# A recurrent attention layer feeding a soft mixture of experts: a reordered unit loop, spread-out tables, and another order at the end

## The chip, the cores and the metric

The kernel runs on one core of a Trainium2 chip. A core has a matrix engine (PE), a vector engine (DVE), a scalar engine (ACT), a general engine (POOL) and a queue engine (SP) that only issues transfers. Each engine works through its own list of instructions in order and waits at semaphores for the others. Sixteen DMA engines move data between the chip's memory (HBM) and the core's on-chip memory (SBUF); transfers are issued by SP or by POOL here. Results of PE land in banks of a small memory (PSUM), which the kernel names T0, T1, Ab, Mb, Yb, Xb and Vb, and are carried off by DVE or ACT.

The metric is the device time of one execution in microseconds (us), the median of several runs. For the kernel before it is 124.12 us over 6 runs (123.98 to 125.6).

## The reference, cut to what matters

The first half is a recurrent attention with a decaying state. `w` is the decay per head and channel, `u` a bonus for the current position. The second half takes the result as tokens, mixes them softly into 32 slots, sends four slots through each of eight experts, and mixes the slots' results back to the tokens.

```
# B, H, S, D = 4, 8, 768, 48;  N, Dm, E, F = 3072, 384, 8, 1024;  32 slots
for t in range(S):
    cur = einsum('bhd,bhe->bhde', u * k[t], v[t])
    y[t] = einsum('bhd,bhde->bhe', r[t], state + cur)
    state = w * state + einsum('bhd,bhe->bhde', k[t], v[t])
x = y as (3072, 384)
logits = x @ phi                           # (3072, 32)
d = softmax of logits over the 3072 tokens # dispatch
slot_input = d.T @ x                       # 32 slots, 4 of each expert
slot_out[e] = relu(slot_input[e] @ w1[e]) @ w2[e]
c = softmax of logits over the 32 slots    # combine
out = c @ slot_out                         # (3072, 384), float32
```

## The kernel before

**Units and iterations.** A unit is one batch and one pair of heads: 4 x 4 = 16 units. The sequence of 768 positions is cut into six chunks of 128, three in each half, so that there are 32 half-units. The main loop `for i in range(-5, nH)` works on half-units; `mu` is i // 2, and odd and even iterations do different things. It is software pipelined: in iteration i one finds the output of half-unit i (`y_pe`, `y_evac`), the diagonal products and the state of half-unit i+1 (`a_pe`, `mask_f`, `m_pe`, `z_evac`), the reordering of v for half-unit i+2 (`v_pe`, `v_evac`), and the preparation of unit mu+2 and of unit mu+3.

**What a unit needs.** POOL multiplies k and r (float32, as loaded) by tables W of powers of the decay (`scale`, L228; unit 0 on DVE). PE transposes the six blocks of k into bank T0 in the even iteration and those of r into bank T1 in the odd one (`t_pe`, L235). ACT carries them off as kT and rT (`t_evac`, L241). PE transposes kT back into T0 (`b_pe`, L247), and DVE carries that off as kn (`b_evac`, L252). DVE multiplies r from T1 by kT as `prod` (`prod_f`, L257), which is needed for the term with u. PE multiplies kT by rT into bank Ab (`a_pe`, L299), and DVE masks that to the causal triangle as AT (`mask_f`, L304). PE forms the state of three chunks and, behind it, the sums with u into bank Mb (`m_pe`, L314 to L329). DVE carries the state off as Z, masked to the two heads' blocks with `bmask` (`z_evac`, L343); for the first half of a unit also as Z0, multiplied by the decay over 384 positions (L339); and multiplies v by the sums as dv (L345). PE adds AT by v, rT by Z, and dv in bank Yb (`y_pe`, L355 to L368), and ACT writes that to x (`y_evac`, L375).

**Routing.** Once a batch is done, `route` takes it through the mixture in the following iterations: transposes of x, logits, their exponential Le, the dispatch sums (`disp`, L425 and L429) in a corner of bank T1, which DVE adds to `acc` in the same iteration (`disp_ev`, L434 and L436), and the transposed exponentials LexpT.

**Order.** All instructions go through `O(...)`, which keeps the order of the program on each engine. Nothing is planned: what the source says first is what an engine does first. Memory hazards become semaphore waits by themselves.

**Transfers.** SP issues k, r and v of batches 0 and 1 in pieces of two heads, then phi, then batch 2, and in iteration 3 batch 3, which goes into the buffer of batch 0. POOL issues the expert weights (`load_w`) from iteration 13 on, as `W_AT` says, between its `scale` steps: w1 of the eight experts, then w2. A weight of 1.5 MB in float32 is converted to bfloat16 on its way. w2 goes to the buffers of batches 1 and 2; that of the last expert comes in three pieces.

**Tables.** `tt` (DVE, L182) and `ex` (ACT, L186) make the eight tables W, one for k or r and a pair of heads; four of them before the loop, the rest in its first iterations by `T_AT`. POOL clears `bmask`, `ones`, `ucol`, `Le`, `uns` ahead of the loop and forms `ucol` from w and u.

**The end.** After the loop come the logits of the last half batches, the first layer of the experts (L594), its transposes (L617), the row sums of the combining softmax in three parts (`row_sums`, L608 and L610), the second layer with all four experts of a group in one pass (L627), the scaling to `so` (L631, L632), and 24 products with LexpT, each carried off by DVE or ACT in turn (L646 to L650) and written out in groups of 1, 1, 2, 4, 4, 4, 4, 4 blocks of 128 tokens (L652).

Of the kernel before, what the change touches and what calls it, by code (L numbers as in the profile page):

```python
# [9 lines left out]
def kernel(  # L10
# [87 lines left out]
    warm = LexpT[:, 2048:2560]  # L98
    wu = cst.tile([8, 128], f32, name="wu")
    wu3 = wu[:].rearrange("q (e s) -> q e s", s=64)  # L100
    phi_f = cst.tile([128, nM, ES], f32, name="phi_f")
    O(act.preload_act_table_set("natural_log_exp_and_others"))
    O(sp.dma_start(out=w_row, in_=w.rearrange("(o h) d -> o (h d)", o=1)))
    O(dve.memset(wu[:], 1.0))
    O(dve.memset(warm, 0.0))
    O(dve.memset(one_f, 1.0))
    O(pool.dma_start(out=wu3[0:4, :, 0:D], in_=w.rearrange("(q e) d -> q e d", e=2)))
    O(pool.dma_start(out=wu3[4:8, :, 0:D], in_=u.rearrange("(q e) d -> q e d", e=2)))
# [9 lines left out]
    def load_batch(b, step):  # L118
        for h0 in range(0, H, step):
            load_kr(0, k, b, h0, h0 + step)  # L120
            load_kr(1, r, b, h0, h0 + step)
            load_v(b, h0, h0 + step)
# [3 lines left out]
    O(sp.dma_start(out=phi_f[:], in_=moe_phi.rearrange("(mo p) s -> p mo s", p=128)))  # L126
# [10 lines left out]
    def keep_warm(n, bank=Yb, data=None):  # L137
        data = warm if data is None else data
        for _ in range(n):
# [5 lines left out]
    ident_f = cst.tile([128, 128], f32, name="ident_f")  # L145
    O(pool.memset(ident_f[:], 0.0))
    O(pool.affine_select(out=ident_f[:], in_=ident_f[:], compare_op=ALU.not_equal, fill=1.0, base=0,
# [5 lines left out]
                         pattern=[[-1, QW]], channel_multiplier=JV))  # L153
    mask_ut = cst.tile([128, 128], f32, name="mask_ut")
# [14 lines left out]
    O(dve.tensor_copy(ident[:], ident_f[:]))  # L169
# [7 lines left out]
    spread(Xb, 0, P2)  # L177
    W = [cst.tile([128, nQ, J, P2], f32, name=f"W{j}") for j in range(2)]
# [14 lines left out]
    tt(0, 1)  # L193
    tt(1, 1)
    ex(0, 1)
    ex(1, 1)
    bmask = cst.tile([128, P2], f32, name="bmask")
    ones = cst.tile([128, 128], bf, name="ones")
    ucol = cst.tile([128, nQ, 2], bf, name="ucol")
    Le_t = [cst.tile([128, L, 128], bf, name=f"Le{j}") for j in range(2)]  # L200
    uns = cst.tile([128, nM, 2, EG, 32], bf, name="uns")
    O(pool.memset(bmask[:], 0.0))
    O(pool.memset(bmask[0:64, 0:D], 1.0))
    O(pool.memset(bmask[64:128, D:P2], 1.0))
    O(pool.memset(ones[:], 1.0))
    O(pool.memset(ucol[:], 0.0))
    for t in Le_t:
        O(pool.memset(t[:], 0.0))
    O(pool.memset(uns[:], 0.0))
    O(pe.transpose(Mb[:, 0:8], wu[:], ident_f[0:8, 0:8]))  # L210
    wuT = cst.tile([128, 8], f32, name="wuT")
    O(dve.tensor_copy(wuT[:], Mb[:, 0:8]))
    O(pool.tensor_mul(ucol[0:64, :, 0], wuT[0:64, 0:4], wuT[0:64, 4:8]))
    O(pool.tensor_mul(ucol[64:128, :, 1], wuT[64:128, 0:4], wuT[64:128, 4:8]))
    wT = cst.tile([128, nQ], f32, name="wT")
    O(act.activation(out=wT[:], in_=wuT[:, 0:4], func=AF.Ln))
    O(act.activation(out=wT[:], in_=wT[:], func=AF.Exp, scale=float(T)))
    phi_s = cst.tile([128, nM, ES], bf, name="phi_s")
    acc = cst.tile([128, NA], f32, name="acc")
    st = {}  # L220
# [111 lines left out]
    def z_evac(i):  # L332
        m, b, q, g, n = at(i)
        dv = wk.tile([128, L * 2, D], bf, name="dv", bufs=2)
        st["dv", i] = dv
        if g == 0:
            Z0 = wk.tile([128, P2], bf, name="Z0", bufs=2)
            st["Z0", m] = Z0
            O(dve.scalar_tensor_tensor(out=Z0[:], in0=Mb[:, 2 * P2:3 * P2], scalar=wT[:, q:q + 1],  # L339
                                       in1=bmask[:], op0=ALU.mult, op1=ALU.mult))  # L340
        Z = wk.tile([128, 2, P2], bf, name="Z", bufs=2)
        st["Z", i] = Z
        O(dve.tensor_mul(Z[:], Mb[:, 0:2 * P2].rearrange("p (c e) -> p c e", c=2),  # L343
                         bmask[:, None, :].to_broadcast([128, 2, P2])))
        O(dve.tensor_mul(dv[:], st["v", i][:].rearrange("p c e d -> p (c e) d"),  # L345
                         Mb[:, 288:288 + 2 * L, None].to_broadcast([128, L * 2, D])))

    def y_pe(i):
# [9 lines left out]
        for c in range(L):  # L358
            if c == 0:
                if g == 0:  # L360
                    continue
                z = st["Z0", m][:]
            else:
                z = Z[:, c - 1, :]
            t = slice((g * L + c) * C, (g * L + c + 1) * C)
            O(pe.matmul(Yb[:, c * P2:(c + 1) * P2], rT[:, t], z, start=False, stop=False,  # L366
                        skip_group_check=True))
# [24 lines left out]
    def xt_ev(n, c, xt=None, eng=None):  # L392
        xT = wk.tile([128, Dm], bf, name="xT", bufs=4)
# [46 lines left out]
    def route(i, part):  # L440
# [6 lines left out]
        if part == 1:  # L447
            if done is not None:
                disp(done, ds_p)
                disp_ev(done, ds_p)  # L450
# [12 lines left out]
        if s < 2 * L:  # L463
            xt_ev(*ch[s])

    W_AT = {13: 1, 14: 1, 15: 1, 16: 1, 18: 1, 19: 1, 21: 1, 22: 1, 23: 1, 25: 1, 26: 5}
    T_AT = {-4: [(dve, 0, 2), (dve, 1, 2), (act, 0, 2)], -3: [(act, 1, 2), (dve, 0, 3)],
            -2: [(act, 0, 3)], -1: [(dve, 1, 3), (act, 1, 3)]}
    nw = 0
    n0, n1 = nG - 2, nG - 1  # L470
    Wf = [t[:].rearrange("p q j d -> p (q j d)") for t in W]
    xs = Wf[0].bitcast(bf)[:, 2 * F:2 * F + 2 * L * Dm].rearrange("p (n m c t) -> p n m c t", n=2, m=nM, c=L)
# [20 lines left out]
    for i in range(-5, nH):  # L493
# [4 lines left out]
        if odd == 0 and 0 <= mu + 1 < nU:  # L498
            prod_f(mu + 1)
# [11 lines left out]
        if 0 <= i + 1 < nH:  # L511
            m_pe(i + 1)
            z_evac(i + 1)
        if odd and 0 <= mu + 3 < nU:
            scale(mu + 3, 0)
# [3 lines left out]
        if 0 <= mu + 2 < nU:  # L519
# [3 lines left out]
            if odd:  # L523
# [11 lines left out]
        for eng, j, q in T_AT.get(i, ()):  # L535
            (tt if eng is dve else ex)(j, q)
        if i == 3:
            load_batch(3, H)
        if i == 4:
            for mi in range(nM):  # L540
                O(dve.tensor_copy(phi_s[:, mi, :].rearrange("p (j g s) -> p g j s", g=2, s=Spe),
                                  phi_f[:, mi, :].rearrange("p (g j s) -> p g j s", g=2, s=Spe)))
# [63 lines left out]
    def row_sums(a, z):  # L606
        for i in range(a, z):
            O(pe.matmul(Mb[:, i:i + 1], LexpT[:, i:Nn:nN], ones[:, 0:1],  # L608
                        start=(i == a), stop=(i == z - 1), skip_group_check=True))
        O(dve.reciprocal(rsr[:, a:z], Mb[:, a:z]))  # L610
# [4 lines left out]
    for g in range(2):  # L615
# [4 lines left out]
        if g == 0:  # L620
            row_sums(0, 8)
    SO = [Xb[:, 0:HD], Yb[:, 0:HD]]
    for g in range(2):
        for y in range(nF):
            for x in range(2):
                for j in range(EG):
                    O(pe.matmul(SO[x][32 * j:32 * j + 32, :], hT[g][:, y, 32 * j:32 * j + 32],  # L627
                                w2_of(g * EG + j)[:, y, x * HD:(x + 1) * HD],
                                start=(g == 0 and y == 0), stop=(g == 1 and y == nF - 1), skip_group_check=True))
    so = cst.tile([128, Dm], bf, name="so")  # L630
    O(dve.tensor_scalar_mul(so[:, 0:HD], SO[0], csr[:, 0:1]))  # L631
    O(act.activation(out=so[:, HD:Dm], in_=SO[1], func=AF.Copy, scale=csr[:, 0:1]))  # L632
    row_sums(8, 16)
# [3 lines left out]
    sizes = [1, 1, 2, 4, 4, 4, 4, 4]  # L637
    obuf = ([raw[0][:, 16 * Dm:17 * Dm], raw[0][:, 17 * Dm:18 * Dm], Wf[0][:, 0:2 * Dm], Wf[1][:, 0:4 * Dm]]
            + [raw[0][:, x * 4 * Dm:(x + 1) * 4 * Dm] for x in range(4)])
    i = 0  # L640
    for gi, sz in enumerate(sizes):
        o_s = obuf[gi][:, 0:sz * Dm].rearrange("p (n m) -> p n m", m=Dm)
        i0 = i
        for j in range(sz):
            op = ob[i % 6][:, 0:Dm]
            O(pe.matmul(op, LexpT[:, i:Nn:nN], so[:], start=True, stop=True))  # L646
            if i % 2 == 0:
                O(dve.tensor_scalar_mul(o_s[:, j, :], op, rsr[:, i:i + 1]))  # L648
            else:
                O(act.activation(out=o_s[:, j, :], in_=op, func=AF.Copy, scale=rsr[:, i:i + 1]))  # L650
            i += 1
        O((sp, pool)[gi % 2 if gi > 1 else 0].dma_start(out=out_v[:, i0:i, :], in_=o_s))  # L652
        if gi == 2:
            row_sums(16, nN)
# [30 lines left out]
```

## Time and profile before

| What | Value |
|---|---|
| Median of 6 runs | 124.12 us (123.98 to 125.6) |
| The profiled execution's own time | 125.6 us |
| Its span, first to last instruction | 123.8 us |
| PE busy | 99.4 us (80%) |
| DVE busy | 98.6 us (80%) |
| ACT busy | 84.1 us (68%) |
| POOL busy | 62.2 us (50%) |
| DMA: mean rate over the span | 257 GB/s |
| HBM read, written | 39.38 MB, 4.72 MB |

The profile is one execution. Its page gives busy times of the engines, the span in 40 slices with a digit of busy share for each, the chain of work that ended last, and groups of instructions by line. Matmuls are pipelined and their ends are modelled, so that a PE that looks busy isn't at its peak; the distance from one start to the next says more. Times below count from the start of the span. The profiled execution was 1.5 us slower than the median, and 1.8 us of its time lie outside the span.

### The profile page before, as it was taken

How to read it: one execution, taken by the hardware profiler on the slowest of the kernel's cores; microseconds unless marked ns; L12 is line 12 of the kernel's file. 1: busy time of each engine (PE TensorE's matmuls, PEld its weight loads, DVE VectorE, ACT ScalarE, POOL GpSimd, SP SyncE). 2: the span in 40 equal slices, each digit the busy share in tenths (PEclk: the TensorE clock that was granted, in tenths of full speed). 3: DMA queues.
4: the chain of work that ended last, by engine and by line, in shares of the span. 5: the costliest groups of instructions: out<-in, count | busy, mean ns of one | idle time of the engine just before them, and what ended most of it. 6: DMA issues, size and time to landing. Idle time of an engine off the chain costs nothing.

```text
span 123.8 us, 4329 instructions
## 1 busy us (share of the span) xinstructions
PE 99.4 (80%) x1784; PEld 79.8 (64%) x1785; DVE 98.6 (80%) x200; ACT 84.1 (68%) x176; POOL 62.2 (50%) x75
## 2 busy tenths in 40 slices
PE   5596948998988998989899898989979799994000
PEld 1245736786867977879787797877868549962000
DVE  1999998899999999898999999999978235597000
ACT  4379946588777878896979888788858253496000
POOL 5879999995556878496677759110000000012100
PEclk9999997699999999999999999999999999999755
DMA  2999999999999999999999999999999991059992
GB/s 62 300 365 374 374 371 368 361 390 358 289 379 372 307 210 220 218 210 214 216 218 210 218 214 215 214 218 216 215 212 216 207 182 26 5 216 393 405 413 97
DMA packets 21093, 31.79 MB, mean 257 GB/s; under 512 B 1361, under 2 KB 18258, under 8 KB 21074
## 3 DMA queue, kind: packets, MB, share of 16 engines
q0 software_dynamic: 3088, 14.95, 54.7%
q1 hardware_dynamic: 17986, 16.57, 39.7%
q8 instruction: 14, 0.23, 0.7%
q14 instruction: 5, 0.04, 0.1%
HBM read 39.38 MB, written 4.72 MB: 356 GB/s over the span
## 4 chain that ended last, share of the span: by engine, by line
DVE 37%; PE 29%; issue 12%; DMA 5%; ACT 4%; SPq 3%; POOL 2%; DVEq 1%; POOLq 0%; ACTq 0%
DVE prod L257 11%; DVE AT L304 8%; DVE dv L345 6%; DVE Z L343 5%; DMA raw<-in_k_dram 5%; PE Vb L284 4%; DVE raw L648 3%; PE Yb L368 3%; PE Mb L325 3%; POOL kr L228 2%; PE T L235 2%; PE T L425 2%; PE T L247 2%; SPq L111 1%; DVE kn L252 1%
## 5 line engine op out<-in xcount | busy, mean ns | idle before, releaser
L228 POOL TENSOR_TENSOR kr<-raw,W 128x576 bf16<-128x576 f32 x30 | 43.3, 1458 | 15.3 <-PE T L235 11.8
L304 DVE TENSOR_TENSOR AT<-Ab,mask_ut 128x768 bf16<-128x768 f32 x32 | 30.4, 949 | 1.0 <-PE Ab L299 1.0
L284 PEld LDWEIGHTS <-Q 128*128 128x128 bf16 x288 | 15.8, 99 | 3.6 <-issue 2.7
L284 PE MATMUL Vb<-v_bf,Q 128*128 128x96 bf16 x288 | 17.7, 207 | 0.0
L235 PE MATMUL T<-ident,kr 128*128 128x128 bf16 x192 | 16.7, 227 | 1.0 <-POOL kr L228 1.0
L241 ACT COPY rT<-T 128x768 bf16<-128x768 bf16 x16 | 12.8, 800 | 6.2 <-PE T L235 2.8
L241 ACT COPY kT<-T 128x768 bf16<-128x768 bf16 x16 | 12.8, 800 | 4.7 <-PE T L235 4.5
L375 ACT CAST x<-Yb 128x288 bf16<-128x288 f32 x32 | 13.1, 410 | 3.2 <-PE Yb L368 3.0
L257 DVE TENSOR_TENSOR prod<-T,kT 128x768 bf16<-128x768 bf16 x16 | 15.1, 947 | 0.0
L652 POOL DMA_DIRECT2D out_dram<-W x1 | 0.5, 541 | 28.2 <-DVE raw L648 28.2
L345 DVE TENSOR_TENSOR dv<-vn,Mb 128x288 bf16<-128x288 bf16 x32 | 14.2, 443 | 0.0
L235 PEld LDWEIGHTS <-kr 128*128 128x128 bf16 x192 | 12.3, 101 | 1.9 <-POOL kr L228 1.3
L290 ACT CAST vn<-Vb 128x288 bf16<-128x288 f32 x32 | 13.1, 410 | 0.6 <-PE Vb L284 0.2
L366 PE MATMUL Yb<-Z,rT 128*128 128x96 bf16 x80 | 10.4, 205 | 3.3 <-DVE Z L343 3.3
L299 PE MATMUL Ab<-rT,kT 64*128 64x128 bf16 x192 | 11.1, 222 | 1.6 <-DVE AT L304 1.6
L325 PE MATMUL Mb<-vn,kn 128*128 128x96 bf16 (+2 forms) x80 | 11.5, 242 | 0.0
L343 DVE TENSOR_TENSOR Z<-Mb,bmask 128x192 bf16<-128x192 f32 x32 | 11.1, 347 | 0.0
L355 PE MATMUL Yb<-vn,AT 128*128 128x48 bf16 x192 | 10.4, 186 | 0.0
L368 PE MATMUL Yb<-dv,ident 128*128 128x288 bf16 x32 | 9.2, 289 | 1.4
L270 ACT CAST v_bf<-raw 128x576 bf16<-128x576 f32 x15 | 10.1, 676 | 0.0
L252 DVE COPY kn<-T 128x768 bf16<-128x768 bf16 x16 | 8.9, 555 | 1.3 <-PE T L247 0.4
L355 PEld LDWEIGHTS <-AT 128*128 128x128 bf16 x192 | 7.0, 97 | 3.3 <-issue 0.2
(141 smaller groups left out, 209.6 us busy)
## 6 DMA issues: line engine op xcount, KB each, us to landing
w_all<-in_moe_w_dram POOLq DMA_DIRECT2D x8, 768.0 KB, 9.7
raw<-in_moe_w_dram POOLq DMA_DIRECT2D x7, 768.0 KB, 14.1
raw<-in_k_dram SPq DMA_DIRECT2D x8, 288.0 KB, 6.0
raw<-in_r_dram SPq DMA_DIRECT2D x8, 288.0 KB, 5.9
raw<-in_v_dram SPq DMA_DIRECT2D x8, 288.0 KB, 6.1
raw<-in_k_dram SPq DMA_DIRECT2D x2, 1152.0 KB, 10.7
raw<-in_r_dram SPq DMA_DIRECT2D x2, 1152.0 KB, 10.1
raw<-in_v_dram SPq DMA_DIRECT2D x2, 1152.0 KB, 11.4
```

The lines of the kernel that those rows point to most:

```text
L228: O(eng.tensor_mul(kr[:, j].rearrange("p j (h s) -> p j h s", s=64)[:, :, :, 0:D], src, W[j][:, q].rearrange("p j (h d) -> p j h d", h=2)))
L235: O(pe.transpose(bank[:, x * C:(x + 1) * C], kr[:, j, x, :], ident[:]))
L241: O(act.copy(t[:].rearrange("p (s j) -> p s j", j=J), bank[:, 0:S].rearrange("p (j s) -> p s j", j=J)))
L257: O(dve.tensor_mul(pr[:].rearrange("p (s j) -> p s j", j=J), T1[:, 0:S].rearrange("p (j s) -> p s j", j=J), st["kT", m][:].rearrange("p (s ...
L284: O(pe.matmul(Vb[:, c * P2:(c + 1) * P2], Q3[:, o:o + C], vb[:, :, g, j, :], start=(j == 0), stop=(j == JV - 1)))
L290: O(act.copy(vn[:].rearrange("p c e d -> p (c e d)"), Vb[:, 0:L * P2]))
L304: O(dve.tensor_mul(AT[:], Ab[:, :, 0:T].rearrange("p e (c t) -> p e c t", c=L), mask_ut[:, None, None, :].to_broadcast([128, 2, L, C])))
L325: O(pe.matmul(o, kn[:, g * L + c, :], vc, start=first, stop=True, skip_group_check=True))
L343: O(dve.tensor_mul(Z[:], Mb[:, 0:2 * P2].rearrange("p (c e) -> p c e", c=2), bmask[:, None, :].to_broadcast([128, 2, P2])))
L345: O(dve.tensor_mul(dv[:], st["v", i][:].rearrange("p c e d -> p (c e) d"), Mb[:, 288:288 + 2 * L, None].to_broadcast([128, L * 2, D])))
L355: O(pe.matmul(Yb[:, o:o + D], AT[:, e, c, :], vn[:, c, e, :], start=first, stop=False, skip_group_check=True))
L375: O(act.copy(st["x", n][:, :, q * P2:(q + 1) * P2], Yb[:, 0:L * P2].rearrange("p (c e) -> p c e", c=L)))
```

## The change

- **Order in the loop.** `prod_f(mu+1)` moves from ahead of `y_pe` to behind `z_evac`, so that DVE does AT, Z, dv, prod in an even iteration where it did AT, prod, Z, dv. From iteration 1 on, `b_pe` and `b_evac` (kn) of an odd iteration move ahead of the transposes of r.
- **State.** The masks become a table `zt` of 4 x 3 x 96 columns, whose third block is multiplied by the decay wT on ACT. One DVE instruction of 288 columns makes Z and Z0 in the first half of a unit; the separate one for Z0 is gone.
- **Dispatch sums.** For all but the last, `disp` uses T0 or T1 by the iteration's parity, and `disp_ev` follows in the next iteration, behind AT.
- **Tables.** Two pairs of heads' tables that stood ahead of the loop are made in iterations -4 to 1. `ucol` is formed by DVE in iteration -3. `ones` and `Le` are cleared by POOL in iteration 2, `uns` (now in W[1]) in iteration 28. `phi_s` moves from DVE to ACT. The two small loads of w and u by POOL stand behind the building of `ident_f` and `Q3`. `ident_f` and `phi_f` lie in the unused end of LexpT. `xT` has two buffers where it had four.
- **Weights.** `W_AT` starts in iteration 14 with two weights. Ahead of them POOL copies one column of v of batch 3 to `guard`, and so waits until heads 0 to 5 of it have landed; the load of v of batch 3 is cut into heads 0 to 5 and 6 to 7.
- **The end.** All row sums are taken before the second half of the second layer. The second layer runs group 0, then experts 4 to 6, then expert 7 alone, with unused matmuls (`busy`) between. The first two output blocks are halved between DVE and ACT, and the groups are 1, 1, 2, 2, 2, 4, 4, 4, 4 blocks.

The core of the diff:

```diff
+    zt = cst.tile([128, nQ, 3, P2], f32, name="zt")
+    O(dve.memset(zt[:], 0.0))
...
     tt(0, 0)
     tt(1, 0)
     spread(Vb, P2, H * D)
     ex(0, 0)
     ex(1, 0)
-    tt(0, 1)
-    tt(1, 1)
-    ex(0, 1)
-    ex(1, 1)
...
+    O(pool.memset(zt[0:64, :, :, 0:D], 1.0))
+    O(pool.memset(zt[64:128, :, :, D:P2], 1.0))
...
-            O(dve.scalar_tensor_tensor(out=Z0[:], in0=Mb[:, 2 * P2:3 * P2], scalar=wT[:, q:q + 1],
-                                       in1=bmask[:], op0=ALU.mult, op1=ALU.mult))
-        Z = wk.tile([128, 2, P2], bf, name="Z", bufs=2)
-        st["Z", i] = Z
-        O(dve.tensor_mul(Z[:], Mb[:, 0:2 * P2].rearrange("p (c e) -> p c e", c=2),
-                         bmask[:, None, :].to_broadcast([128, 2, P2])))
+            st["Z0", m] = Z[:, 2, :]
+        O(dve.tensor_mul(Z[:], Mb[:, 0:x * P2].rearrange("p (c e) -> p c e", c=x), zt[:, q, 0:x, :]))
...
             if done is not None:
-                disp(done, ds_p)
-                disp_ev(done, ds_p)
+                if i < nH - 4:
+                    ds = (ds_t, ds_p)[i % 2]
+                    disp(done, ds)
+                    pend.append((done, ds))
+                else:
+                    disp(done, ds_p)
+                    disp_ev(done, ds_p)
...
-    W_AT = {13: 1, 14: 1, 15: 1, 16: 1, 18: 1, 19: 1, 21: 1, 22: 1, 23: 1, 25: 1, 26: 5}
-    T_AT = {-4: [(dve, 0, 2), (dve, 1, 2), (act, 0, 2)], -3: [(act, 1, 2), (dve, 0, 3)],
-            -2: [(act, 0, 3)], -1: [(dve, 1, 3), (act, 1, 3)]}
+    pend = []
+    W_AT = {14: 2, 15: 1, 16: 1, 18: 1, 19: 1, 20: 1, 22: 1, 23: 1, 25: 1, 26: 5}
+    T_AT = {-4: [(tt, 0, 1), (tt, 1, 1), (ex, 0, 1), (tt, 0, 2)], -3: [(ex, 1, 1), (ex, 0, 2)],
+            -1: [(tt, 1, 2), (ex, 1, 2)], 0: [(tt, 0, 3), (ex, 0, 3)], 1: [(tt, 1, 3), (ex, 1, 3)]}
+    Z_AT = {-3: 0, -1: 1, 1: 2, 2: 3}
...
         if 0 <= i + 1 < nH:
             a_pe(i + 1)
             mask_f(i + 1)
-        if odd == 0 and 0 <= mu + 1 < nU:
-            prod_f(mu + 1)
+        if pend:
+            disp_ev(*pend.pop())
...
             m_pe(i + 1)
             z_evac(i + 1)
+        if odd == 0 and 0 <= mu + 1 < nU:
+            prod_f(mu + 1)
+        if odd and i > 0 and mu + 2 < nU:
+            b_pe(mu + 2)
+            b_evac(mu + 2)
...
-            if odd:
+            if odd and i < 0:
                 b_pe(mu + 2)
                 b_evac(mu + 2)
...
+        if i == 2:
+            O(pool.memset(ones[:], 1.0))
+            for t in Le_t:
+                O(pool.memset(t[:], 0.0))
         if i == 3:
-            load_batch(3, H)
+            load_batch(B - 1, H, 2)
...
+        if i == min(W_AT):
+            O(pool.tensor_copy(guard[:], raw_of(2, B - 1)[:, 0:1]))
         for _ in range(W_AT.get(i, 0)):
             load_w(nw)
...
+    second(0, range(EG))
+    row_sums(8, nN)
+    row_recip(8, nN)
+    busy(2)
+    second(1, range(EG - 1))
+    busy(1)
+    second(1, (EG - 1,))
...
-    sizes = [1, 1, 2, 4, 4, 4, 4, 4]
+    sizes = [1, 1, 2, 2, 2, 4, 4, 4, 4]
...
+            if i < 2:
+                emit(i, 2 * i, o_s[:, j, :], 0, HD, dve)
+                emit(i, 2 * i + 1, o_s[:, j, :], HD, Dm, act)
             else:
-                O(act.activation(out=o_s[:, j, :], in_=op, func=AF.Copy, scale=rsr[:, i:i + 1]))
+                emit(i, i + 2, o_s[:, j, :], 0, Dm, (dve, act)[i % 2])
```

## The prediction

> **What bounds the kernel now.** I read the slices of the page first, then one unit of the loop on DVE and PE by time, then the transfers by window, then the end.
>
> ```profile
> DVE  1999998899999999898999999999978235597000
> PEclk9999997699999999999999999999999999999755
> DMA  2999999999999999999999999999999991059992
> GB/s 62 300 365 374 374 371 368 361 390 358 289 379 372 307 210 220 218 210 214 216 218 210 218 214 215 214 218 216 215 212 216 207 182 26 5 216 393 405 413 97
> ```
>
> The DMA engines are full from slice 1 to slice 31, 3 to 102 us: inputs until about 42 us, then the weights at some 215 GB/s. They rest for about 5 us, then write the output from 108 to 122 us. DVE is full until 95 us.
>
> ```profile
> 60.42 0.95 DVE L304 TENSOR_TENSOR AT<-Ab,mask_ut 128x768 bf16<-128x768 f32 x1
> 61.56 0.32 DVE L339 SCALAR_TENSOR_TENSOR Z<-Mb,wT,bmask 128x96 bf16<-128x96 f32 x1 [0.19 <-PE Mb L329]
> ...
> 62.56 0.56 DVE L252 COPY kn<-T 128x768 bf16<-128x768 bf16 x1
> ...
> 60.20 0.24 PE L366 MATMUL Yb<-Z,rT 128*128 128x96 bf16 x2 [0.23 <-DVE Z L343]
> 60.55 0.28 PE L368 MATMUL Yb<-dv,ident 128*128 128x288 bf16 x1
> ```
>
> This is one unit of 4.97 us (AT at 58.07, again at 63.04). In its even iteration PE stands before Z and dv (its matmul starts are 59.76, 60.20, 60.24, 60.55: 0.4 + 0.27 us lost), because prod (0.95 us) lies ahead of them on DVE. In its odd iteration DVE stands before Mb. They wait for each other in turn.
>
> ```profile
> raw<-in_v_dram SPq DMA_DIRECT2D x1, 1152.0 KB, 11.4
> w_all<-in_moe_w_dram POOLq DMA_DIRECT2D x1, 768.0 KB, 7.2
> raw<-in_moe_w_dram POOLq DMA_DIRECT2D x1, 192.0 KB, 22.3
> ```
>
> These are answers for three windows: v of batch 3 (issued 32.87, landed 44.2), the first weight (40.52, landed 47.7), and the last piece of the last weight (81.52, landed 103.8).
>
> ```profile
> 103.59 2.60 PEld L627 LDWEIGHTS <-W 128*32 128x32 bf16 x128
> 106.16 0.26 PE L627 MATMUL Yb<-raw,W 128*32 128x192 bf16 x4
> 106.38 0.42 DVE L631 TENSOR_SCALAR so<-Xb,csr 128x192 bf16<-128x192 f32 x1 [2.26 <-PE Xb L627]
> 107.33 0.62 DVE L648 TENSOR_SCALAR raw<-T,rsr 128x384 f32<-128x384 f32 x1
> 107.98 1.74 SPq L652 DMA_DIRECT2D out_dram<-raw  x2
> ...
> 109.00:110.00 1.00, 0.98 (x6) 0.69 (x5) 1.00 (x3) 1.00 (x3) 0.00 (x0) 1.00 0.40 141
> 110.00:111.00 1.00, 0.92 (x6) 0.54 (x5) 1.00 (x3) 1.00 (x3) 0.54 (x1) 1.00 0.83 307
> ```
>
> The second layer ends at 106.42, 2.6 us after the last weight landed: the compute chain sets the end, with the weights close behind. From the first output issue (107.98) 15.8 us remain to the end of the span; 4.72 MB at the 406 GB/s of the windows behind would take 11.6. The output starts slowly: the last columns are share and GB/s, 0.40 and 0.83 where full is 1.
>
> **What the Trainium skill says.** "DMA: Bandwidth & Descriptors", Queues, rings and completion order: each DMA engine goes round the queues by packet. The trace agrees: in the window 42 to 43 us, with batch 3 and the first weight both under way, the rate is 241 GB/s, against 365 just before. So starting weights earlier would not have added bandwidth, and starting them late loses it. The same page, Anatomy of one DMA: a POOL-issued transfer has a fixed cost of about 2 us. Here one packet of the first weight had started by 42.0, 1.5 us after its issue; I use that. "TensorE: Matmul & The Clock Gate", Part 1: after an idle window of about 3.4 us the clock is halved. The trace shows 0.50 at 21 to 23 us after PE had stood from 16.6 to 18.3. "TensorEngine Tiling (Array Packing)", Key Properties: column tiles run in parallel. The trace agrees: four matmuls of the second layer start together, the next four 0.083 us later.
>
> **The change, part by part.**
>
> *Loop.* DVE, start to start in this unit: AT 0.87 x 2, prod 0.86, Z 0.26 x 2, dv 0.36 x 2, Z0 0.24, kn 0.48 = 4.56 us. From the sixth AT (27.70) to the thirtieth (88.65) a unit takes 60.95 / 12 = 5.08. After: Z0 goes (-0.24), the wider Z costs +0.10 (96 columns more, by dv at 0.44 for 288 against Z at 0.35 for 192), so 4.42. Dispatch additions (0.25 each, six in twelve units) are 0.12 before and after: 4.54. PE, of 4.97 without its 0.67 of stalls, is 4.30; the dispatch matmuls (about 0.67 with their transposes, six in twelve units) make it 4.6. Now follow the new order. dv to dv is kn + AT (1.35) or prod + AT (1.73), while PE takes about 0.95 from dv to Mb (Yb 0.13, Vb 0.38, Mb 0.32, latency): no wait on either side. prod ends as PE wants it, within 0.1 us. kn's transposes need only kT, which ACT finished an iteration earlier, and T1's next writer comes 0.7 us after prod has read it. A unit is PE's 4.6 to 4.7: 12 x 0.43 = 5.2 us. Bounds: 3 (half the stalls return) to 6.
>
> *Start.* k and r of unit 0 wait for two tables on DVE until 7.62; without those they start when their own are ready, about 6.3: 1.3 us, between 0.3 and 1.7, since later tables now delay AT in iterations 0 to 2. The cleared table zt (1,152 columns; kr's 192 take 0.22, so about 1.2) fits into DVE's idle time from 1.40 to 3.06. POOL's clearing in iteration 2 (1.0) is covered by its lead of some 7 us over PE at unit 4 (done 21.3, used about 29); without cover it costs that 1.0. ACT takes phi_s and zt's third blocks, seven short copies of 0.17 to 0.3, at 75 to 85% busy: nothing. xT with two buffers is read an iteration after its writing: nothing, at worst 0.4 per batch. So the compute chain reaches the end of the loop 6.5 us earlier (3.3 to 7.7).
>
> *Dispatch sums later.* The three waits of PE for prod in that line (1.7 us in all) go; DVE's sum lies between AT and Z, where Mb is not late. It is inside the 5.2.
>
> *Second layer.* The 32 groups of four cost 2.65 us now. After: 16 groups for experts 0 to 3 (1.33), 16 row sums (1.2, by eight at 0.6), three busy matmuls (0.65), 16 groups of three (1.33), 16 single ones (1.33, nothing beside them): 5.85, so 3.2 more. By compute alone it would end at 106.42 + 3.2 - 6.5 = 103.1.
>
> *Weights.* With a faster loop POOL reaches the guard at about 41, and waits. r of batch 3 landed at 40.8; v of six heads is 0.885 MB, 2.45 us at 360 GB/s, so 43.3, or 42.5 if the lag shrinks with the smaller piece: I take 43.0. The issue is at 43.1 where it was at 40.52, the first packet 1.5 later at 44.6. The first weight landed 5.7 us after its first packet, about one of which was shared with batch 3; alone 4.7: 49.3 against 47.7. POOL's further issues run ahead of the 3.7 us that a weight takes. So **all weights land 1.6 us later** (0.8 to 2.6), the last at 105.4. Behind the guard in POOL's queue stands k of unit 10, wanted in iteration 16, two iterations or 4.6 us on: the stall of 2 us is covered; uncovered, it would cost the compute chain those 2 us, which it can spare.
>
> *End.* After the last piece four single matmuls remain: 0.06 + 0.25 + 0.26. The second layer ends at 105.95: **-0.45**. From there to the first issue it was 1.56; with half blocks (0.42 instead of 0.62) and no row sums or reciprocal between, about 1.35: **-0.2**. Smaller groups feed the queues sooner: the start wastes about 2 us of full rate; a second SP issue that again takes 1.3 us leaves a gain of 0.2, without it 0.75: **-0.45**. PE now idles some 2.5 us waiting for the weights, so a halved clock is possible (+0.5 on single matmuls), at a fifth: **+0.1**. Sum **-1.0 us**: 125.6 becomes 124.6 for the profiled execution, and the median, 1.5 below it, 124.1 becomes 123.1.
>
> **The rivals.**
>
> *The weights don't bind* (27%). The guard releases at 42.5 or the weights recover time, so they land at most 0.7 later: second layer 105.0, -1.4, and the end's gains -0.8: 121.9. For it: in the window 42 to 44 the mixed traffic was below full rate, which is time to win. Against: 1.5 us of latency with idle engines.
>
> *The guard costs more than the end gives, slower* (8%). Every us that the weight stream starts late is a us at the end. From 2.6 us on it eats all gains. It needs the guard's release at 44.2, where all of v landed before, and single matmuls on a halved clock: all weights 2.8 later, the second layer's end at 103.84 + 2.8 + 0.57 = 107.2 (+0.8), the clock +0.5, the end's -0.65: 124.8. Each further us that POOL comes late to the guard adds one.
>
> *The loop doesn't speed up* (13%). If new waits replace the old, so that less than 3.7 us is won, compute still sets the end, with 3.2 us more to do in it. At 2 us: second layer 107.6, +1.2, less 0.65: 124.6. For it: PE is already 95% busy by its modelled ends. Against: the start-to-start sums.
>
> **How the numbers follow.** The likeliest case (52%) is 123.1, from 122.2 to 124.1 by the bounds of the weights' start. The range takes in the first rival and nearly all of the third: 121.4 to 124.6. About 1% is what a measurement of this kernel can tell from no change, so 122.9 and 125.4 divide: faster takes the first rival and a third of the likeliest case, 0.45; slower 0.05, from the ends of the second and third rivals; the rest 0.50.
>
> **What would show it.** Loop: AT to AT below 4.75 us per unit, no Z waiting for Mb, no PE waiting for Z. Weights: POOL idle before its first weight on a landing of v; first weight's issue near 43; last landing near 105.4; PE idle in the second layer on weights. End: first output issue near 107.2. Wrong if AT to AT stays at 5, or if the last weight lands by 104 or after 107.

## The result and the profile after

The changed kernel is **slower by 0.7%**: 125.9 us median (124.79 to 127.68, 29 runs) against 124.86 us for the kernel before on the same chips (123.96 to 127.55, 66 runs), ratio 1.007 with a 95% interval of 1.0045 to 1.0094. The medians take in all runs; the ratio leaves out the few that fell in a slower state of the chip, so it isn't quite their quotient. The forecast was 123.1 us, so the sign was wrong. The profiled execution took 126.46 us with a span of 124.7 (before: 125.6 and 123.8).

The slices of the page of the changed kernel, 3.1 us each:

```profile
DVE  6799999999999998999998999996823500199000
...
PEclk9999599999999999999999999999999996799855
DMA  2999999999999469999999999999999997059992
GB/s 80 319 367 371 377 367 367 363 390 349 361 383 361 134 83 215 217 212 213 216 213 216 217 214 214 212 220 216 217 211 216 213 208 144 9 212 384 406 414 99
```

The loop did get shorter: DVE falls from full two slices sooner. But slices 13 and 14 of the DMA row (counted from 0), which were 9 before, are now 4 and 6, and the GB/s there are 134 and 83. The same place by windows of 1 us (the last three columns are TensorE clock, DMA share and GB/s):

```profile
41.00:42.00 1.00, 1.00 (x25) 0.78 (x23) 1.00 (x3) 0.80 (x2) 0.75 (x1) 1.00 0.66 190
42.00:43.00 1.00, 0.98 (x20) 0.78 (x18) 1.00 (x2) 1.00 (x3) 0.00 (x0) 1.00 0.20 60
43.00:44.00 1.00, 1.00 (x19) 0.79 (x20) 1.00 (x4) 0.76 (x3) 0.51 (x2) 1.00 0.05 16
44.00:45.00 1.00, 1.00 (x26) 0.97 (x24) 1.00 (x2) 1.00 (x4) 0.98 (x3) 1.00 0.11 12
45.00:46.00 1.00, 0.97 (x27) 0.88 (x25) 1.00 (x4) 0.72 (x3) 1.00 (x1) 1.00 1.21 117
```

and POOL, by time:

```profile
43.49 0.19 POOL L564 COPY guard<-raw 128x1 f32<-128x1 f32 x1 [1.74 <-DMA raw<-in_v_dram]
43.61 1.18 POOL L135 DMA_DIRECT2D w_all<-in_moe_w_dram  x2
```

POOL stands 1.74 us at the guard, until heads 0 to 5 of v have landed (43.44). The transfer was nearly done long before. The share is 0.20 and then 0.05, less than one engine in sixteen (0.06): most DMA engines have finished and a last one trails. The first weight is issued only then, at 43.61 (before: 40.52), and its first packet starts at 44.93. In the kernel before weights were already queued, and the engines are full in the same windows:

```profile
42.00:43.00 1.00, 1.00 (x26) 0.95 (x23) 1.00 (x2) 1.00 (x3) 1.00 (x2) 1.00 1.16 241
43.00:44.00 1.00, 1.00 (x24) 0.80 (x21) 1.00 (x2) 0.56 (x3) 0.64 (x3) 1.00 1.05 219
```

The first weight and the last piece after the change, issued at 43.61 and 84.72 (a row ends with the size and the us from issue to landing):

```profile
w_all<-in_moe_w_dram POOLq DMA_DIRECT2D x1, 768.0 KB, 7.5
raw<-in_moe_w_dram POOLq DMA_DIRECT2D x1, 192.0 KB, 22.5
```

So the stream of weights starts late, and nothing makes that up: from the first weight's landing to the last piece's it takes 56.12 us before (47.72 to 103.84) and 56.15 after (51.10 to 107.25).

PE at the end, by time:

```profile
101.14 0.26 PE L653 MATMUL Xb<-raw,W 128*32 128x192 bf16 x2
103.56 0.24 PE L653 MATMUL Xb<-raw,W 128*32 128x192 bf16 x1 [2.16 <-DMA raw<-in_moe_w_dram]
...
104.86 0.49 PE L653 MATMUL Xb<-raw,W 128*32 128x192 bf16 x3
105.02 0.49 PE L653 MATMUL Yb<-raw,W 128*32 128x192 bf16 x3
...
105.76 0.61 PE L144 MATMUL Ab<-w_all 128*128 128x512 bf16 x1
```

The second layer starts 5.55 us earlier than before (98.04 against 103.59), then waits for expert 6. After the wait the clock is halved, from 104.1 to 107.5 us: groups start 0.16 us apart where they were 0.083. The third column from the right is the clock:

```profile
104.00:105.00 1.00, 1.00 (x28) 1.00 (x24) 0.00 (x0) 0.00 (x0) 0.00 (x0) 0.54 0.83 149
105.00:106.00 1.00, 1.00 (x17) 0.55 (x10) 0.00 (x0) 0.00 (x0) 0.00 (x0) 0.50 0.40 71
106.00:107.00 1.00, 1.00 (x6) 0.67 (x6) 0.00 (x0) 0.00 (x0) 0.00 (x0) 0.50 0.15 29
```

The second layer ends at 108.36, 1.94 us later than before. From 103.56 on no matmul of it waits for a transfer any more: the four that need the last piece start at 107.86, 0.61 us after it has landed. In this execution the late stream reaches the end through expert 6 and the halved clock.

| us in the span | before | after |
|---|---|---|
| Sixth AT, thirtieth AT (start) | 27.70, 88.65 | 26.60, 82.21 |
| A unit, AT to AT | 5.08 | 4.63 |
| First weight issued, landed | 40.52, 47.72 | 43.61, 51.10 |
| Last piece landed | 103.84 | 107.25 |
| Second layer ends | 106.42 | 108.36 |
| First output issue | 107.98 | 109.59 |
| Span | 123.8 | 124.7 |

### The profile page after: what moved, and what is told of

Same layout as the page of the kernel before. It is cut to its first block, busy times and chain, and to the rows that moved or that the text cites. A ratio compares the mean times of both kernels' runs of the same rounds, so it can differ in the third digit from the quotient of the medians.

```text
span 124.7 us, 4312 instructions
## 1 busy us (share of the span) xinstructions
PE 103.5 (83%) x1788; PEld 82.1 (66%) x1790; DVE 96.3 (77%) x185; ACT 83.3 (67%) x184; POOL 60.8 (49%) x72
## 4 chain that ended last, share of the span: by engine, by line
DMA 40%; PE 23%; DVE 17%; issue 5%; ACT 4%; POOL 2%; POOLq 0%; DVEq 0%; ACTq 0%
DMA raw<-in_moe_w_dram 24%; DMA w_all<-in_moe_w_dram 14%; DVE W L190 4%; DVE prod L257 3%; PE T L235 3%; PE Vb L284 2%; DVE AT L304 2%; DVE kn L252 2%; PE T L247 2%; DMA out_dram<-W 2%; PE Ab L299 2%; PE Xb L653 2%; PE Yb L352 2%; DVE Z L341 2%; DVE dv L342 2%
## 5 line engine op out<-in xcount | busy, mean ns | idle before, releaser
L228 POOL TENSOR_TENSOR kr<-raw,W 128x576 bf16<-128x576 f32 x30 | 42.2, 1429 | 11.7 <-ACT W L194 6.4
L341 DVE TENSOR_TENSOR Z<-Mb,zt 128x288 bf16<-128x288 f32 (+1 forms) x32 | 12.8, 399 | 0.9 <-PE Mb L329 0.2
L138 POOL DMA_DIRECT2D raw<-in_moe_w_dram x10 | 5.4, 548 | 10.5 <-DMA raw<-in_moe_w_dram 6.3
L299 PEld LDWEIGHTS <-kT 64*128 64x128 bf16 x192 | 5.6, 95 | 5.6 <-DVE AT L304 2.0
```

Of the source, the lines that this page charges most:

```text
L228: O(eng.tensor_mul(kr[:, j].rearrange("p j (h s) -> p j h s", s=64)[:, :, :, 0:D], src, W[j][:, q].rearrange("p j (h d) -> p j h d", h=2)))
L299: O(pe.matmul(Ab[:, e, c * C:(c + 1) * C], kT[s, t], rT[s, t]))
L341: O(dve.tensor_mul(Z[:], Mb[:, 0:x * P2].rearrange("p (c e) -> p c e", c=x), zt[:, q, 0:x, :]))
```

## The experiments

Two theories stood at the start. **L**: the start of the weight stream sets the end, and the guard starts it late. **C**: the new end costs the time, by the last expert alone and a halved clock. The kernel before ran beside every group of runs, at medians of 124.63 us (first four kernels below), 125.34 (the next four), and 125.15 or 123.99 (the rest); the ratios are taken against those.

### Without the guard

```diff
-        if i == min(W_AT):
-            O(pool.tensor_copy(guard[:], raw_of(2, B - 1)[:, 0:1]))
```

> The changed kernel without the guard copy (so the computation is the same); weights from iteration 14 as changed. Theory L (the end is set by when the weight stream starts, and the guard starts it late): POOL issues the first weight at about 41.8 instead of 43.6, every weight lands 1.9 us earlier (last near 105.4), and the time falls by about 2 us against the changed kernel, to about 123.0, a little below the kernel before. Theory C (the last expert alone and a halved PE clock cost the time, not the landing): the last weight lands earlier, but the time stays within 0.5 us of the changed kernel.

Measured: 123.77 us (123.51 to 123.98, 8 runs), ratio 0.992 (0.988 to 0.995). The first weight was issued at 41.58 and landed at 48.53, the last piece at 104.85; the clock stayed whole at the end, with waits for pieces of 0.37 and 0.46 us only. The second layer starts at 97.94 us, as in the changed kernel (98.04), so it isn't POOL's own delay at the guard that costs the time. The guard alone turns a gain of 0.8% into a loss of 0.7%.

### Without the guard, weights from iteration 13 as before

```diff
-    W_AT = {14: 2, 15: 1, 16: 1, 18: 1, 19: 1, 20: 1, 22: 1, 23: 1, 25: 1, 26: 5}
+    W_AT = {13: 1, 14: 1, 15: 1, 16: 1, 18: 1, 19: 1, 21: 1, 22: 1, 23: 1, 25: 1, 26: 5}
```

> The changed kernel without the guard and with the weights issued from iteration 13 by the old list. Theory L: first issue near 40.4, last landing near 103.9 as in the kernel before, and another 1.4 us off the time: about 121.6, 2% under the kernel before. If weights issued while batch 3 still loads only share its bandwidth (what the prediction said), the last landing and the time are those of a1_no_guard. Theory C: no change against the changed kernel beyond 0.5 us.

Measured: 122.41 us (122.3 to 123.7, 4 runs), ratio 0.983 (0.974 to 0.992). First weight issued 40.12, landed 47.37; last piece 103.80. The windows that were empty are full:

```profile
41.00:42.00 1.00, 1.00 (x26) 0.87 (x24) 1.00 (x3) 1.00 (x2) 1.00 (x1) 1.00 1.30 352
42.00:43.00 1.00, 0.98 (x20) 0.78 (x18) 1.00 (x3) 1.00 (x4) 0.98 (x3) 1.00 1.06 234
43.00:44.00 1.00, 1.00 (x25) 0.79 (x22) 1.00 (x3) 0.76 (x3) 1.00 (x1) 1.00 1.08 227
```

So of the 3.45 us between the last landings of this kernel and the changed one, 1.05 come from the iteration by which `W_AT` starts later, 2.40 from the guard. No kernel run here was clearly better than this one. This and the run before it lie 0.8 us above L's figures, which started from 124.12 us, where the kernel before took 124.63 on this chip; in ratio L's figures were 0.991 and 0.980.

### The guard in the kernel before

The kernel before with the cut load of v, the new `W_AT` and the guard:

```diff
+            load_v(3, 0, H - 2)
+            load_v(3, H - 2, H)
...
+        if i == min(W_AT):
+            O(pool.tensor_copy(guard[:], raw_of(2, B - 1)[:, 0:1]))
```

> The kernel before with the guard alone: the cut load of v of batch 3, the guard copy and the new list of weights. Theory L: first issue near 43.6, last landing near 107.2, and the second layer, which takes its last matmuls from the last piece, ends near 107.8 instead of 106.4: 125.5. If the old compute chain has room for late weights: 124.1, as the kernel before.

Measured: 127.14 us (125.47 to 127.4, 4 runs), ratio 1.013 (1.003 to 1.024). Slower, as L says, but it does not price the guard. In this profile the loop began 1.1 us later (AT at 14.60, before 13.51), and POOL came to the guard after v had landed (43.24), so there is no wait ahead of it:

```profile
42.84 1.41 POOL L229 TENSOR_TENSOR kr<-raw,W 128x576 bf16<-128x576 f32 x1 [1.05 <-PE T L236]
44.19 0.19 POOL L548 COPY guard<-raw 128x1 f32<-128x1 f32 x1
44.31 1.19 POOL L131 DMA_DIRECT2D w_all<-in_moe_w_dram  x2
```

The last landing at 107.03 and the second layer's end at 107.6 fit L, but the late computing would have ended near there too (106.42 and 1.1). The first weight was issued at 44.31, 0.7 us later than in the changed kernel, and the last piece landed 0.2 earlier, so issue and last landing go together to within about a microsecond only. This run separates little.

### The loop and the start alone

The changed start and loop, with the weights, the undivided v and the end of the kernel before.

> The changed kernel's start and loop with the old list of weights, no guard, and the old second layer, row sums and output. The loop ends 5.5 us earlier as in the changed kernel. Theory L: the last landing (about 103.9) sets the end of the second layer, 104.5 instead of 106.4: about 122.2. If the loop's gain were all hidden, 124.1; if nothing but compute counted, 118.6.

Measured: 123.19 us (122.74 to 124.46, 4 runs), ratio 0.988 (0.979 to 0.996). A unit takes 4.63 us, as in the changed kernel, but the last landing stays at 103.80: a loop 5.3 us shorter gives 1.2% (L's 122.2 was 1.5%), since the rest disappears behind the weights: PE waits for them three times between 99.4 and 103.2 us, for 0.66, 1.65 and 0.39. The new end adds some 0.5% to that (0.983 against 0.988, inside their intervals).

### The guard on a smaller piece

```diff
-            load_batch(B - 1, H, 2)
+            load_batch(B - 1, H, 4)
```

> The changed kernel with v of batch 3 cut into heads 0 to 3 and 4 to 7, so that the guard waits for 0.59 MB instead of 0.88. L: if the release follows the bytes, it comes 0.8 to 1.2 us earlier (42.3 to 42.6), and the first and last landings and the end with it: 124.7 to 125.1. If one trailing DMA engine sets the landing of either piece, the release stays at 43.2 or later and the time at 125.6 to 126. C (the end's order is what costs): 125.9, whatever the release.

Measured: 124.63 us (124.12 to 127.37, 12 runs), ratio 0.996 (0.993 to 1.000), 1.1% better than the changed kernel. The profiled execution of this kernel took 127.28 us, 2.65 more than the median, with the clock halved from 102 to 109 us, so its end isn't used. Its POOL rows show the release 0.64 us earlier:

```profile
42.85 0.19 POOL L564 COPY guard<-raw 128x1 f32<-128x1 f32 x1 [0.99 <-DMA raw<-in_v_dram]
```

Heads 0 to 3 landed at 42.80. At 360 GB/s the 0.295 MB less would be 0.82. In two more profiles with the six heads (the runs with one pass and with PE kept at work, below) POOL's wait ended at 43.20 and 43.22, so of the 0.64 some 0.3 may be chance; the release follows the bytes in part. Last piece 106.35. The starts and ends line up: first issue 41.58, 42.98, 43.61 (no guard, four heads, six heads), last landing 104.85, 106.35, 107.25, median 123.77, 124.63, 125.9 (in ratio 0.992, 0.996, 1.007).

### The last expert not alone

The end of the changed kernel with experts 4 to 7 in one pass, once with the guard and once without it and with weights from iteration 13:

```diff
-    busy(2)
-    second(1, range(EG - 1))
-    busy(1)
-    second(1, (EG - 1,))
+    second(1, range(EG))
```

> The changed kernel with its guard, but with experts 4 to 7 of the second layer in one pass, as before, and without the three unused matmuls between. L (the start of the weight stream sets the end): the last weight still lands near 107.2 us of the span, the second layer ends 0.6 us after it instead of 1.1, and the time falls by 0.3 to 0.7, to 125.2 to 125.6. C (the lone last expert is what the change pays for): the time falls by 1 us or more, to 124.9 or less. If the last expert alone is a gain, as it was meant, the time rises above 125.9.

Measured: 125.7 us (125.49 to 126.31, 7 runs), ratio 1.0067 (1.0028 to 1.0105), the same as the changed kernel's 1.007 and just above L's 125.2 to 125.6. Last piece 106.97; the clock is halved here too.

> The changed kernel without the guard, weights from iteration 13 as before, and experts 4 to 7 in one pass without unused matmuls. L: 122.4 to 122.7, the last weight landing at 103.8 as with the lone expert, because four groups of four (0.33 us) and a drain of 0.26 remain after it against 0.53 measured there. C: 121.5 or less.

Measured: 123.01 us (122.51 to 123.42, 4 runs), ratio 0.985 (0.980 to 0.990), against 0.983 with the lone expert; the time is above L's 122.4 to 122.7, the ratio at its edge (0.986). From the last landing to the first output issue it takes 1.78 us (103.56 to 105.34), with the lone expert 1.77 (103.80 to 105.57). The lone expert neither costs nor gains anything that these runs can tell. C falls as the main cause.

### Weights earlier still

The kernel without the guard, with

```diff
+    W_AT = {11: 1, 12: 1, 13: 1, 14: 1, 15: 1, 17: 1, 19: 1, 21: 1, 22: 1, 24: 1, 25: 1, 26: 4}
```

> The changed kernel without the guard, the weights from iteration 11 (one each in 11 to 15, 17, 19, 21, 22, 24, 25, four in 26). If an earlier start adds no bandwidth (the engines are full with batch 3 until 41.5 us), the first weight only takes from batch 3: last landing 103.5 to 104.0, time 122.3 to 122.7, or more if a late batch 3 holds up the loop. If the mixed stretch has spare room beyond what weights from iteration 13 fill: last landing 103.0 or less, 121.3 to 122.0.

Measured: 122.67 us (122.31 to 123.07, 4 runs), ratio 0.9825 (0.978 to 0.987), equal to the start in iteration 13. The first weight is issued 2.4 us earlier (37.76) and lands only 0.4 earlier (46.97); the last piece lands at 103.96. What the weights take, batch 3 gives: heads 0 to 5 of its v landed at 55.87 instead of 43.0. An early start gains nothing once the engines are full; a late one loses what they stand idle.

### Keeping PE at work during the wait

```diff
-    busy(2)
+    busy(12)
```

> The changed kernel with its guard, and twelve unused matmuls instead of two ahead of experts 4 to 6 (ten more, 2.2 us at full clock, where PE waited 2.4 us for a weight). H (the wait for late weights lets the clock halve, and the halved matmuls then end later than the last weight): no clock of 0.5 between 103 and 108 us, the second layer ends 0.5 to 0.6 us after the last landing, and the time is 125.0 to 125.3, the lower part of what the changed kernel showed (124.8 to 127.7). Against it: the weights alone set the end, so 125.6 to 126.2; or the extra matmuls come too late and add their own time, above 126.2.

Measured: 125.32 us (124.78 to 126.23, 20 runs), ratio 1.0025 (0.9999 to 1.0051). PE has no long wait left:

```profile
100.63 2.75 PE L144 MATMUL Ab<-w_all 128*128 128x512 bf16 x11
103.31 0.26 PE L653 MATMUL Xb<-raw,W 128*32 128x192 bf16 x2
103.84 0.24 PE L653 MATMUL Xb<-raw,W 128*32 128x192 bf16 x1 [0.28 <-DMA raw<-in_moe_w_dram]
```

```profile
104.00:105.00 1.00, 1.00 (x43) 1.00 (x40) 0.00 (x0) 0.00 (x0) 0.00 (x0) 1.00 0.71 126
105.00:106.00 1.00, 0.75 (x18) 0.61 (x12) 0.00 (x0) 0.00 (x0) 0.00 (x0) 1.00 0.30 58
```

The clock is whole from 100 us to the end of the second layer, which ends 0.5 us after the last landing (106.94), where the changed kernel needed 1.1. The time is 0.4% lower, with intervals that just touch, so the size is loose. The changed kernel's 29 times leave a gap between 125.29 and 125.90, with 14 below and 15 above, and its profile is one of those above. Of the 20 runs here 16 are below 125.7, and four are still above 125.8. The clock granted over the whole execution fits that: 0.966 on average in the 14, 0.947 in the 15, and one stretch of 3.4 us at half clock takes 0.014 off it. But the two groups lie 1.2 us apart, more than this end explains, and each kernel has one profile. So the halved clock is part of the loss, about 0.5 us as far as these runs can tell; the late weights are the main part, and what else divides the changed kernel's runs is open.

### Which part of the loop does it

Four kernels from the one before: prod behind Z and dv; kn ahead of r's transposes; both; both with the dispatch sums taken up an iteration later.

```diff
-        if odd == 0 and 0 <= mu + 1 < nU:
-            prod_f(mu + 1)
...
             z_evac(i + 1)
+        if odd == 0 and 0 <= mu + 1 < nU:
+            prod_f(mu + 1)
```

> The kernel before with one edit: the products prod behind Z and dv instead of ahead of the output products. If PE's stalls for Z and dv in the even iteration (0.67 us a unit) are what the loop loses: a unit from AT to AT takes 4.65 to 4.8 us instead of 5.08, and the loop ends 3.5 to 5 us earlier; the time falls to 122.7 to 123.5, since the weights' landing at 103.8 takes over. If the loop is DVE's own work (4.56 us plus Z0), 4.9 to 5.05.

> The kernel before with one edit: from iteration 1 on the transposes of kT and their eviction kn ahead of the transposes of r. If prod's place alone carries the loop's gain: 5.0 to 5.1 us a unit, no change in the time. If DVE's wait for Mb in the odd iteration counts as much: 4.75 to 4.9.

> The kernel before with both edits, prod behind Z and kn ahead of r's transposes. If these two are all of the loop's gain: 4.63 to 4.68 us a unit, as in the changed kernel (4.635). If the merged Z and the dispatch sums taken up later carry a part: 4.75 to 4.9. Time 122.3 to 123.2 either way, bound by the last landing near 103.8.

> The kernel before with prod behind Z and dv, kn ahead of r's transposes, and the dispatch sums taken up an iteration later from T0 or T1 in turn. If the sums' place is what the two moves alone lacked (l3_both: units with dispatch sums 5.9 to 6.0 us, those without 4.54): units with sums fall to 5.3 to 5.5, the ones without stay at 4.54, the mean to 4.70 to 4.76, and the merged Z (0.12 a unit) is all that is left to the changed kernel's 4.635. If the merged Z is what frees the units with sums: they stay at 5.7 or more and the mean at 4.85 or more.

Each ran once, in its profile, so only the distances in the trace are read. A unit is from one AT to the next but one. The second column of numbers follows one batch, from the unit with a dispatch sum on:

| kernel | a unit, mean of 12 | four units from the one with a sum | time, us |
|---|---|---|---|
| before | 5.08 | 5.49, 5.21, 4.97, 4.97 | |
| prod moved | 5.24 | 6.12, 4.70, 5.06, 4.91 | 127.83 |
| kn moved | 4.96 | 5.34, 4.99, 4.92, 4.83 | 123.39 |
| both | 4.98 | 5.96, 4.84, 4.93, 4.79 | 124.6 |
| both, sums later | 4.77 | 4.99, 4.79, 4.71, 4.54 | 123.24 |
| the changed kernel | 4.63 | 5.25, 4.66, 4.58, 4.42 | |

None of the four means lies in a range that was written down for it. Prod alone gains nothing in the steady loop: its four units take 20.79 us against 20.64, and the higher mean of 5.24 comes from the first unit counted, 6.76 us, in which the copies to phi_s take 2.3 us on DVE and PE then runs at half clock. Kn alone gains 0.12 us a unit, both together no more. Rows of DVE in the kernel with prod alone, and then rows of PE and of DVE in the one with both, show what stands in the way:

```profile
62.76 0.56 DVE L252 COPY kn<-T 128x768 bf16<-128x768 bf16 x1 [0.42 <-PE T L247]
```

```profile
69.32 0.39 PE L425 MATMUL T<-Le,x 128*128 128x32 bf16 x9 [0.89 <-DVE prod L257]
```

```profile
68.31 0.95 DVE L257 TENSOR_TENSOR prod<-T,kT 128x768 bf16<-128x768 bf16 x1
69.81 0.26 DVE L436 TENSOR_TENSOR acc<-acc,T 128x97 f32<-128x97 f32 x1 [0.54 <-PE T L429]
70.27 0.96 DVE L304 TENSOR_TENSOR AT<-Ab,mask_ut 128x768 bf16<-128x768 f32 x1 [0.21 <-PE Ab L299]
```

In the first, DVE waits for kn's transposes, which PE does behind r's. In the second kernel that wait is gone, but PE waits 0.89 us for prod before it can put the dispatch sums into T1, where prod still reads r; DVE in turn waits for the sums, and stands with AT behind them. Put into T0 or T1 in turn and taken up later, they hold up less, and the four units fall from 20.52 to 19.03 us. The rest of the way to 4.63 seems to lie in two things that were not run by themselves: the merged Z (quiet units: 4.54 to 4.42), and phi_s, three copies that cost DVE about 1 us once, in iteration 4 (that unit: 5.52 against 4.41), and are on ACT in the changed kernel. So prod's move is worth something only with the sums out of its way. Of the times, the first was 4 us above what was expected: its thirtieth AT is only 0.3 us later than in the kernel before, but then PE waits 1.43 us for prod and runs at half clock from 93.0 to 96.4, and computing sets the end (second layer 108.8, last landing 103.7). The kernel with kn alone, where none was expected, gained some 1.8 us against the median beside it, as far as one run can tell.

## Why the prediction was wrong

**The step that failed** is "all weights land 1.6 us later (0.8 to 2.6)". The last piece landed 3.4 us later (3.1 in the two later profiles with the same guard), outside the bounds, and at 107.25, after the 107 that the prediction itself named as a sign of being wrong. By its terms:

- The guard's release: 43.0 predicted from 0.885 MB at 360 GB/s and a lag; 43.44 measured. The lag did not shrink with the piece: r had landed at 40.97, and 2.45 us more give 43.42. The Trainium skill's page "DMA: Bandwidth & Descriptors", Why a DMA increments its semaphore by 16 and not by 1, says that a transfer's up to 16 engines finish independently and that only the full count means that all has landed. The trace agrees: the share fell below 0.7 in the window from 41 us, and the landing came at 43.44. That was the first 0.45 us.
- From issue to first packet: 1.5 taken, 1.3 measured.
- From first packet to the first weight's landing: 4.7 taken, as 5.7 less "about one of which was shared with batch 3". It was 6.2, on engines with nothing else to do (117 GB/s in the first microsecond, 195 in the next). In the kernel before, the packets of batch 3 took 0.57 us of the engines' time from 42 to 44 us, and having the engines to itself did not give the stream even that back: from the weights' first packet to the last landing it takes 61.85 us before and 62.3 after. Nor is it that two weights are issued at once: the kernel without the guard does that too, and there the first took 5.6. This **1.5 us is the greater part of the error**.
- Between the first and the last landing no time came back, as assumed.

That mis-sizing has one root. The prediction priced the overlap of weights and batch 3 as a loss for the weights, and the first rival called the traffic from 42 to 44 us "below full rate". But the engines' share there is 1.16 and 1.05: they are full, and the lower GB/s are what weights move by themselves. Weights that are queued while batch 3 ends fill the engines that finish early, and that is lost when they wait for a landing. "Starting weights earlier would not have added bandwidth" held for starts before iteration 13, as the run from iteration 11 shows; "starting them late loses it" was priced too low.

**Behind it, the second layer's end**: 0.57 us after the last landing predicted, 1.11 measured. The halved clock was given "a fifth" and so 0.1 us. In the profiles of the new loop the clock stayed whole at the end where the last piece landed by 104.85, and was halved where it landed at 106.35, 106.97 and 107.25, unless PE was kept at work. So it went with the lateness. The Trainium skill's page "TensorE: Matmul & The Clock Gate", Part 1, speaks of an idle window of about 3.4 us; here PE stood for 2.16 us by the wait's row, and 0.5 us later the clock was halved, for 3.4 us. The prediction's own example was no longer, 1.7 us (16.6 to 18.3). The measurement decides: a shorter stand can do. The run with twelve unused matmuls puts about 0.5 us on it.

**Right**: the loop's 5.2 us (5.34 measured), the chain reaching the loop's end 5.6 us earlier (6.5 taken, within 3.3 to 7.7), 1.35 us from the second layer's end to the first issue (1.23), the output's ramp (0.77 shorter, 0.45 predicted). Carried through the sum with the measured terms, +1.85 for the landing, +0.54 for the second layer's end, -0.12 and -0.32 for the last two, and -0.1 since the clock's chance is now a measured term, the predicted 124.6 us of the profiled execution becomes 126.45; it took 126.46. The sum has to close, since every term in it is measured; it shows that none was left out.

**Right in size, wrong in reason**: the loop. The prediction took the place of prod as the cause and PE's 4.6 to 4.7 us as the new bound. The quiet units take 4.42 us, which is to 0.01 the prediction's sum of DVE's instructions without dispatch. One such unit of the changed kernel on DVE, by time:

```profile
56.69 0.95 DVE L304 TENSOR_TENSOR AT<-Ab,mask_ut 128x768 bf16<-128x768 f32 x1
57.56 0.45 DVE L341 TENSOR_TENSOR Z<-Mb,zt 128x288 bf16<-128x288 f32 x1
57.92 0.44 DVE L342 TENSOR_TENSOR dv<-vn,Mb 128x288 bf16<-128x288 bf16 x1
58.28 0.55 DVE L252 COPY kn<-T 128x768 bf16<-128x768 bf16 x1
58.75 0.95 DVE L304 TENSOR_TENSOR AT<-Ab,mask_ut 128x768 bf16<-128x768 f32 x1
59.62 0.35 DVE L341 TENSOR_TENSOR Z<-Mb,zt 128x192 bf16<-128x192 f32 x1
59.88 0.45 DVE L342 TENSOR_TENSOR dv<-vn,Mb 128x288 bf16<-128x288 bf16 x1
60.24 0.95 DVE L257 TENSOR_TENSOR prod<-T,kT 128x768 bf16<-128x768 bf16 x1
61.11 0.95 DVE L304 TENSOR_TENSOR AT<-Ab,mask_ut 128x768 bf16<-128x768 f32 x1
```

No row has a wait: DVE is the bound, and PE is fed in time. "The dispatch sums later" was booked at nothing of its own, "inside the 5.2"; the runs show that without it the two moves give 0.10 of the 0.45 us a unit.

**Right by luck**: the start. Its 1.3 us seem to be there, the sixth AT being 1.1 earlier, but the first AT is only 0.12 earlier. In the kernel with prod moved and nothing else, which has the old start, the sixth AT comes at 26.08, before the changed kernel's 26.60. So the order made this gain, not the spread-out tables.

**The rivals.** The second came in: the guard costs more than the end gives, and decides from 2.6 us of lateness. At 2.8 us it gave 124.8, 0.7 above the median it started from; at the measured 3.4 it gives 1.3, and the medians of the result lie 1.0 apart. It got 8%, because a lateness above 2.6 was taken for two mishaps together, where the halved clock went with the lateness itself. The first rival needed weights at most 0.7 us later (its sum takes the end's gains at 0.8, where the others take 0.65; with that it would be 122.05); the third, a slow loop, is refuted.

## What to carry to other kernels

When a steady stream of transfers sets the end, look at when it starts and at how many DMA engines stand idle then; a wait for a landing in front of the stream costs the tail of the slowest DMA engine, the issue, and the ramp of the new transfer, one after the other. A faster loop ahead of such a stream brings only what the stream's landing leaves, here 1.2% for 5.3 us. And a move in the order can be worth nothing until another one is made: price the waits that the moved instruction leaves behind on the same bank.

## What the runs showed of the hardware

- The last part of a load trails. With nothing else queued the DMA share fell from 1.13 in the window 40 to 41 us to 0.66, 0.20 and 0.05 before the landing at 43.44. At the end the packets come one at a time, eight from 43.2 to 43.4 us, as one engine would send them. Which engine trails, and why, the trace doesn't tell.
- A weight converted from float32 on its way took 7.5 us from issue to landing on idle engines (43.61 to 51.10; 6.55 in the kernel before with the guard), no less than the 7.2 in the kernel before behind other traffic, and about 3.7 each once the stream runs.
- With weights from iteration 11 the two queues took turns by packet, not by byte: from 43 to 57 us 499 packets of the weights ran and 492 of batch 3, but 2.75 MB against 0.28 MB, since a packet of v has 576 bytes and one of a weight up to 6,144. So heads 0 to 5 of v landed 12.9 us later (55.87 against 43.0) when weights came 2.4 us earlier.
- A wait of 2.16 us on PE was enough for 3.4 us of half clock. Three waits of 0.66, 1.65 and 0.39 us in the kernel with the loop alone were not. The stretches at half clock that ended within a profile lasted 3.4 us or twice that (6.8 in the runs with one pass and with the guard on four heads).
